# Four chunks' decays broadcast by TensorE, 256-column idle products in shorter gaps, and a new order of issue

## The chip, the cores and the metric

The kernel runs on one core of a Trainium2 chip. The metric is the device time of one execution in microseconds (us), of which three are given for the kernel before. TensorE is called PE here, VectorE DVE, ScalarE ACT, GpSimd POOL; SP issues nearly all DMAs.

## The reference

Three stages follow one another on 4 batches of 768 tokens with 8 heads of 32. Cut to what matters:

```python
# 1: chunked state space scan (per head; N = 16 states, D = 32)
cum = np.cumsum(log_a, axis=-1); L = np.exp(cum_i - cum_j) * causal   # decays
y  = (C @ B.T * L) @ x + (C @ state) * np.exp(cum)
state = decay_full * state + sum_j decay_from_j * B_j x_j
# 2: x of all heads side by side, 256 wide
xn = (x - mean) / sqrt(var + 1e-6) * g_ln
x  = x + relu(xn @ w_ch1) @ w_ch2                  # 256 -> 1024 -> 256
# 3: mix along the sequence with rank 32, then a second such network
u = x + (x.T @ U @ V).T
out = u + relu(u @ w_ch1) @ w_ch2
```

## The kernel before, in words

**Work.** Tokens are handled in chunks of 128: 6 chunks per batch, numbered k = 0 to 23 over all batches. In the first two batches a chunk is cut in two halves of 64 tokens (`NS = (2, 2, 1, 1)`). The two networks take the tokens in groups of 256 (chunks 0 and 1 of a batch) and 512 (chunks 2 to 5).

**A chunk's chain** (function `chunk`). The decays a of chunk k must stand on all partitions as the tile `lt`; `bc` brings them there. A scan on DVE (line 677) turns `lt` into the products of decays. PE forms C·B (`cb`, two chunks at a time), DVE multiplies both (`mm`, line 701), DVE or POOL scales B by the last decay (`bw`, line 719), PE forms the chunk's state (`sps`), DVE carries it on (`gst`) and masks it (`stm`, line 805), and PE puts all together in `yps` (lines 754 and 763). ACT and DVE split that into a high and a low part (`yhl`), PE transposes a copy (`tps`), and ACT takes mean and variance from it.

**How the decays get to all partitions.** Lines 464 to 479 load the rows of chunks 2 to 23 once (`rows`), clip them on DVE (line 462), let POOL set the first of each chunk to zero, and store them in DRAM as `arows`. For every chunk from the third on, `bcast` loads from there with a broadcast: two DMAs of 64 partitions in the first batches. `lt` has three buffers, one of which first holds `rows`. For chunks 0 and 1 (`if k < 2`, line 622) another way is taken: two small loads put the raw rows on a few partitions (tile `r`), DVE clips and splits them in two float32r parts (`rh`), and one pair of products per chunk with a selecting matrix `selr` puts them on all partitions in PSUM (`bcp`, line 615), where the scan reads them.

**Weights.** They come as 64-bit words (`raw`, 512 KB a piece; three buffers). ACT and DVE make float32 of them (ACT lines 268 and 369, DVE line 373 twice: the merges) and split them into a high and a low part. For the first matrix of network 1, PE also takes out the mean with four products `pc` (line 396) and one more (line 409). A token group times a high and low weight needs six products `hps` (line 928); ACT and DVE split its relu (`hh` line 935, `hl` line 939), and six or twelve products `acc` (lines 953 and 959) follow.

**What sets the order.** Everything is one list per engine, written out by a planner (`Plan.issue`): each item has a cost, its predecessors and a due time, and the planner plays them through with constants for cost (`LAT`, `RATE`, ...), shifts of due times (`SHIFT`) and `T0`, `PER` for the networks. The engines then run these lists in order; what an item really waits for is a semaphore. A queue is never overtaken: a DVE instruction that waits holds all that stand behind it.

**Idle products.** Where the planner sees a gap on PE it puts in products of zeros (`filler`, in the trace `dummy`), which wait for nothing and give nothing:

```python
while n != "dummy" and now < WARM[2] and t - now > WARM[3]:
    self.filler()
```

`WARM` gives the planned time from which they may stand, the time up to which they are costed double, the time after which there are none, and the gap above which they are put in.

Of the kernel before, what the change touches and what calls it, by code (L numbers as in the profile page):

```python
# [8 lines left out]
F32 = mybir.dt.float32  # L9
F32R = mybir.dt.float32r  # L10
# [3 lines left out]
ALU = mybir.AluOpType  # L14
# [3 lines left out]
C = 128  # L18
NC = S // C
XW = DM + H * N  # L20
NK = B * NC
# [3 lines left out]
WARM = (1.0, 8.0, 60, 1.0)  # L25
EARLIEST = {'warm': 62.0, ('cb', 0, 0): 6.0, (('w1', 0, 0), 'ld'): 3.2}
# [4 lines left out]
FIRST = [('bc0', 0), ('bcl', 0), ('sel', 0), ('sel', 1), 'cst0', ('ra', 0, 0), ('rcb', 0, 0), ('stk', 0), ('xb', 0), (('w1', 0, 0), 'ld'), 'cst', 'rows',  # L31
# [4 lines left out]
POOL = {'rac': (), 'bw': (3, 4), 'stm': (4, 2)}  # L36
PE_SPLIT = ()
# [6 lines left out]
LAT, PER, T0, NEAR, SWITCH, STAY = 0.298, 1.0526, 11.79, 0.2, 0.046, 3.07  # L44
# [9 lines left out]
RATE, FLIGHT = 282, 8  # L54
# [5 lines left out]
SHIFT = dict(zip("rows w0 w1 w2 ra0 ra chunk0 chunk".split(), [-0.37, 1.36, 0.67, 13.48, -4.54, -9.02, -1.53, -2.91]))  # L60
# [16 lines left out]
class Plan:  # L77
# [35 lines left out]
    def issue(self):  # L113
# [45 lines left out]
        while left:  # L159
# [21 lines left out]
            if eng == "PE":  # L181
                now = max(free[eng], WARM[0])
                while n != "dummy" and now < WARM[2] and t - now > WARM[3]:
                    self.filler()
                    step = dict(words=2, cost=0.216 if now > WARM[1] else 0.43)
                    now = max(now, self.fetched(step))
                    self.ran(step, now)
                    now += step["cost"]
                t = max(t, self.fetched(it))
                self.ran(it, t)  # L190
# [38 lines left out]
def mamba_ffn_mixer(ctx: ExitStack, tc: tile.TileContext, a_rows, a_rep, cbT, xb,  # L229
# [37 lines left out]
    def copy(out, in_, **kw):  # L267
        A.activation(out=out, in_=in_, func=AF.Copy, **kw)  # L268
# [25 lines left out]
    stk = {}  # L294
# [280 lines left out]

    def chunk(k):
# [30 lines left out]
        def ld_first_rows():  # L607
            for j in range(2):
                load(out=pair["r"][32 * j:32 * j + 2], in_=a_rows[j:j + 1].rearrange("k (i x) -> (k i) x", i=2))
# [12 lines left out]
        if k < 2:  # L622
            if k == 0:
                pair["r"] = y_p.tile([128, 512], F32, tag="uhl0", name="r2")
                pair["sel"] = y_p.tile([128, 2, C], F32R, tag="uhl1", name="selr")
                pair["h"] = y_p.tile([128, 2, 512], F32R, tag="yhl1", name="rh")
                sl_ = pair["sel"]
                add(("bcz", k), "DVE", 0.3, lambda: V.memset(pair["r"], 0.0), due=-3e3)
                add(("selz", k), "DVE", 0.17, lambda: V.memset(f32(sl_)[:, 1, :], 0.0))
                add(("sel", 0), "ACT", act(C), lambda: copy(sl_[:, 0, :], sel), ["cst0", "table"])  # L630
                add(("sel", 1), "ACT", act(C), lambda: copy(sl_[32:64, 1, :], sel[0:32]), ["cst0", "table", ("selz", k)])
                add(("bc0", k), "SP", sp(2, 8), ld_first_rows, [("bcz", k)])
                add(("bc1", k), "DVE", dve2(512), lambda: clip(pair["r"]), [("bc0", k)])
# [6 lines left out]
        else:  # L640
            gone = [x for j in ((0, 1) if k in (3, 4) else (k - 3,)) for x in
# [29 lines left out]
        def scan(hf):  # L671
            if k == 0:
                pair[2] = att_p.tile([128, 1024], F32, tag="lt", name="lt", bufs=3)
            if k < 2:
                lt[k] = pair[2][:, 512 * k:512 * (k + 1)]
            t = lt[k][:, hf * 512:(hf + 1) * 512]
            V.tensor_tensor_scan(t, pair[k] if k < 2 else t, eye, 0.0, op0=ALU.mult, op1=ALU.add)  # L677
# [24 lines left out]
        for hf in range(parts):  # L702
            add(("scan", k, hf), "DVE", scn(512), lambda hf=hf: scan(hf), [("bc", k), ("eye", ns)] + [("scan", 0, 0)] * (k == 1),
                frees=[("bc", k)] * (k < 2))
# [403 lines left out]
    def bank():  # L1108
# [4 lines left out]
    plan.filler = lambda: P.matmul(dummy[0], zeros[:, :C], zeros.rearrange("p (o i) -> p o i", o=1).to_broadcast([128, 2, 2 * C]),  # L1113
                                   start=True, stop=True)
# [52 lines left out]
```

## Time and profile before

| | us |
|---|---|
| time, median of 3 runs (371.94, 375.89, 377.66) | 375.89 |
| the profiled execution's own time | 375.81 |
| its span, first to last instruction | 374.0 |
| PE busy | 361.4 (97%) |
| DVE busy | 244.0 (65%) |
| ACT busy | 169.5 (45%) |
| mean granted share of the TensorE clock | 0.982 |

The profile is of one execution. The 1.8 us between its time and its span lie before the first and after the last instruction. A busy PE is not PE at its peak: a product that runs at half the clock is busy twice as long.

### The profile page before, as it was taken

The numbers are of one execution on the slowest core, as the hardware profiler recorded it, in microseconds if no ns is written. First come the engines' busy times: TensorE is split into PE (matmuls) and PEld (weight loads), VectorE is DVE, ScalarE is ACT, GpSimd is POOL, SyncE is SP. The second block draws the span as 40 slices with busy tenths as digits, with TensorE's granted clock in tenths as the row PEclk, the third lists the DMA queues.
The fourth block names the chain that finished last, engine by engine and source line by source line (L and its number), as shares of the span: only waits on it lengthen the run. The fifth ranks groups of instructions, "written<-read, shape, count | busy, mean of one in ns | idle before, by whom it ended". The sixth has DMA issues, their size and how long they took to land.

```text
span 374.0 us, 8463 instructions
## 1 busy us (share of the span) xinstructions
PE 361.4 (97%) x3377; PEld 306.8 (82%) x3377; DVE 244.0 (65%) x523; ACT 169.5 (45%) x473; POOL 9.3 (2%) x27
## 2 busy tenths in 40 slices
PE   7898799999999999999999999999999999999996
PEld 3476698989878789899887689998978788998896
DVE  6869789999995693896462796458952742434242
ACT  3473784677962642433432551225442551244221
POOL 4001100000100000000000000000000000000000
PEclk9599989999999999999999999999999999999999
DMA  5858862746380425791220435019200100000010
GB/s 149 248 169 224 261 191 60 205 137 202 106 322 20 144 78 154 215 355 40 64 85 0 147 101 152 4 46 270 92 26 0 58 3 0 2 0 30 0 57 30
DMA packets 31973, 41.58 MB, mean 111 GB/s; under 512 B 4170, under 2 KB 21370, under 8 KB 31934
## 3 DMA queue, kind: packets, MB, share of 16 engines
q1 hardware_dynamic: 31502, 40.67, 35.7%
q8 instruction: 27, 0.44, 0.5%
q10 hardware_dynamic: 432, 0.37, 0.3%
q14 instruction: 12, 0.10, 0.1%
HBM read 33.07 MB, written 7.95 MB: 110 GB/s over the span
## 4 chain that ended last, share of the span: by engine, by line
PE 84%; DVE 5%; DMA 5%; ACT 1%; issue 1%; SPq 1%; POOL 1%; DVEq 0%; ACTq 0%; POOLq 0%
PE hps L928 34%; PE acc L959 18%; PE acc L953 15%; PE pc L396 2%; DMA xt<-in_xb 2%; PE yps L742 2%; PE yps L754 2%; PE cb L694 2%; PE ups L1040 2%; DMA rows<-in_a_rows 1%; PE tps L856 1%; DMA raw<-in_w 1%; SPq L253 1%; PE gps L1001 1%; PE yps L763 1%
## 5 line engine op out<-in xcount | busy, mean ns | idle before, releaser
L939 DVE SCALAR_TENSOR_TENSOR hl<-hps,hh 128x256 fp32r<-128x256 f32 (+1 forms) x128 | 70.6, 552 | 92.9 <-ACT hh L935 92.7
L935 ACT ACTIVATE hh<-hps 128x256 fp32r<-128x256 f32 (+1 forms) x128 | 62.6, 489 | 138.8 <-PE hps L928 130.8
L928 PE MATMUL hps<-yhl,w 128*128 128x512 f32 (+1 forms) x384 | 79.1, 344 | 1.2 <-ACT w L268 0.6
L928 PE MATMUL hps<-uhl,w 128*128 128x256 f32 (+1 forms) x384 | 77.7, 339 | 0.0
L959 PE MATMUL acc<-hh,w 128*128 128x512 f32 (+1 forms) x256 | 73.8, 340 | 0.0
L953 PE MATMUL acc<-w,hh 128*128 128x256 f32 x384 | 73.1, 286 | 0.2 <-DVE w L271 0.2
L928 PEld LDWEIGHTS hps<-yhl,w 128*128 128x128 f32 x384 | 59.9, 192 | 10.1 <-ACT w L268 1.3
L928 PEld LDWEIGHTS hps<-uhl,w 128*128 128x128 f32 x384 | 60.8, 189 | 8.4 <-ACT u L268 0.4
L953 PEld LDWEIGHTS acc<-w,hh 128*128 128x128 f32 x384 | 62.0, 192 | 3.8 <-issue 0.8
L953 PE MATMUL acc<-w,hl 128*128 128x256 f32 x192 | 54.6, 284 | 0.0
L959 PEld LDWEIGHTS acc<-hh,w 128*128 128x128 f32 x256 | 46.1, 189 | 5.9 <-issue 1.0
L677 DVE TENSOR_TENSOR_SCAN lt<-lt,eye 128x512 f32<-128x512 f32 x34 | 41.0, 1214 | 4.3 <-DMA lt<-arows 4.3
L959 PE MATMUL acc<-hl,w 128*128 128x512 f32 (+1 forms) x128 | 43.2, 337 | 0.1
L953 PEld LDWEIGHTS acc<-w,hl 128*128 128x128 f32 x192 | 37.0, 192 | 0.0
L959 PEld LDWEIGHTS acc<-hl,w 128*128 128x128 f32 x128 | 24.2, 189 | 2.6 <-DVE hl L939 0.3
L701 DVE TENSOR_TENSOR mm<-cb,lt 128x512 f32<-128x512 f32 x36 | 23.6, 683 | 1.5 <-PE cb L694 1.0
L268 ACT ACTIVATE w<-raw 128x512 f32<-128x512 f32 (+2 forms) x19 | 12.2, 643 | 16.6 <-DMA raw<-in_w 10.2
L268 ACT ACTIVATE yhl<-yps 128x128 fp32r<-128x128 f32 x48 | 11.1, 274 | 15.6 <-PE yps L763 8.6
L271 DVE TENSOR_TENSOR yhl<-yps,yhl 128x128 fp32r<-128x128 f32 x48 | 11.6, 285 | 4.8 <-ACT yc L268 2.2
L369 ACT ACTIVATE raw<-raw,half 128x512 int32<-128x512 uint16 (+2 forms) x19 | 13.9, 734 | 0.0
L373 DVE SCALAR_TENSOR_TENSOR w<-w,raw 128x512 int32<-128x512 int32 (+2 forms) x19 | 12.3, 655 | 1.6 <-PE pc L409 1.1
L373 DVE SCALAR_TENSOR_TENSOR w<-raw,w 128x512 int32<-128x512 int32 (+2 forms) x19 | 12.3, 650 | 0.0
(111 smaller groups left out, 357.3 us busy)
## 6 DMA issues: line engine op xcount, KB each, us to landing
raw<-in_w SPq DMA_DIRECT2D x16, 512.0 KB, 5.0
lt<-arows SPq DMA_DIRECT2D x12, 512.0 KB, 5.3
stk<-st SPq DMA_DIRECT2D x48, 96.0 KB, 2.7
st<-sh SPq DMA_DIRECT2D x8, 384.0 KB, 4.3
xt<-in_xb SPq DMA_DIRECT2D x14, 192.0 KB, 4.1
lt<-arows SPq DMA_DIRECT2D x20, 128.0 KB, 3.7
out<-u SPq DMA_DIRECT2D x8, 256.0 KB, 2.1
xt<-in_xb SPq DMA_DIRECT2D x20, 96.0 KB, 3.4
```

Of the source, the lines that this page charges most:

```text
L268: A.activation(out=out, in_=in_, func=AF.Copy, **kw)
L271: eng.tensor_tensor(out=out, in0=in0, in1=in1, op=ALU.subtract)
L369: A.activation(out=words(0), in_=cell["r"][:rows, :2 * n].bitcast(U16).rearrange("p (n w) -> p n w", w=4)[:, :, 1], func=AF.Identity, scal ...
L373: V.scalar_tensor_tensor(out=cell["t"].bitcast(I32), in0=a(), scalar=scalar, in1=b(), op0=op, op1=ALU.bitwise_or)
L396: P.matmul(p[:, o * 256:(o + 1) * 256], (gd if o == k else gm)[:, k, :], t()[:, k, :], start=(o == k == 0), stop=False, skip_group_check=True)
L677: V.tensor_tensor_scan(t, pair[k] if k < 2 else t, eye, 0.0, op0=ALU.mult, op1=ALU.add)
L701: V.tensor_tensor(out=mm_[k][:, s_], in0=cbp[k, hf], in1=lt[k][:, s_], op=ALU.mult)
L928: P.matmul(p[:, :n], w[:, k, fs], x[:, k, :], start=(i == 0), stop=(i == 5))
L935: A.activation(out=hh[:, :n], in_=hps[l, key, f][:, :n], func=AF.Relu)
L939: V.scalar_tensor_tensor(out=hl[:, :n], in0=hps[l, key, f][:, :n], scalar=0.0, in1=f32(hh[:, :n]), op0=ALU.max, op1=ALU.subtract)
L953: P.matmul(p, x[:, t * C:(t + 1) * C], w[:, f, :], start=(f == 0 and i == 0 and t % 2 == 0), stop=(f == NF - 1 and i == 2), skip_group_che ...
L959: P.matmul(accs[l, key][d][:, :n], w[:, f, ds_], x[:, :n], start=(f == 0 and i == 0), stop=(f == NF - 1 and i == 2))
```

## The change

One load of eight rows of 512 replaces the two small loads; tile `r` then holds chunks 0 to 3, and `selr` selects for four chunks (two ACT copies out of an identity matrix instead of two out of a stored pattern; the memset of `selr` goes). Chunks 2 and 3 take their decays from `bcp` too: four more products, and their four broadcast DMAs go. The pairs (0, 1) and (2, 3) each share a buffer of `lt`, and `before` names the chunks that must be done before a buffer is used again. The idle products have 256 columns instead of 512, fill gaps above 0.6 us (planned) instead of 1.0, and end at 28 us planned instead of 60. The constants of cost and due times are others, so all lists have another order.

```diff
-WARM = (1.0, 8.0, 60, 1.0)
-EARLIEST = {'warm': 62.0, ('cb', 0, 0): 6.0, (('w1', 0, 0), 'ld'): 3.2}
+WARM = (1.0, 6.0, 28, 0.6)
+EARLIEST = {'warm': 30.0, ('cb', 0, 0): 6.0, (('w1', 0, 0), 'ld'): 3.2}
...
+ROWS = 4
...
-LAT, PER, T0, NEAR, SWITCH, STAY = 0.298, 1.0526, 11.79, 0.2, 0.046, 3.07
+LAT, PER, T0, NEAR, SWITCH, STAY = 0.287, 1, 13.09, 0.115, 0.056, 3.07
...
-RATE, FLIGHT = 282, 8
+RATE, FLIGHT = 251, 8
...
-SHIFT = dict(zip("rows w0 w1 w2 ra0 ra chunk0 chunk".split(), [-0.37, 1.36, 0.67, 13.48, -4.54, -9.02, -1.53, -2.91]))
+SHIFT = dict(zip("rows w0 w1 w2 ra0 ra chunk0 chunk".split(), [-1.78, -6.02, 1.38, 12.04, -3.04, -11.46, -1.31, -2.87]))
...
-                    step = dict(words=2, cost=0.216 if now > WARM[1] else 0.43)
+                    step = dict(words=2, cost=0.109 if now > WARM[1] else 0.216)
...
+    def before(k):
+
+        tiles = [()] + [(j, j + 1) for j in range(0, ROWS, 2)] + [(j,) for j in range(ROWS, NK)]
+        at = next(i for i, t in enumerate(tiles) if k in t)
+        return tiles[at - 3] if at >= 3 else ()
...
         def ld_first_rows():
-            for j in range(2):
-                load(out=pair["r"][32 * j:32 * j + 2], in_=a_rows[j:j + 1].rearrange("k (i x) -> (k i) x", i=2))
+            load(out=pair["r"][:2 * ROWS], in_=a_rows[:ROWS].rearrange("k (i x) -> (k i) x", i=2))
...
-        if k < 2:
+        if k < ROWS:
...
-                add(("selz", k), "DVE", 0.17, lambda: V.memset(f32(sl_)[:, 1, :], 0.0))
-                add(("sel", 0), "ACT", act(C), lambda: copy(sl_[:, 0, :], sel), ["cst0", "table"])
-                add(("sel", 1), "ACT", act(C), lambda: copy(sl_[32:64, 1, :], sel[0:32]), ["cst0", "table", ("selz", k)])
-                add(("bc0", k), "SP", sp(2, 8), ld_first_rows, [("bcz", k)])
-                add(("bc1", k), "DVE", dve2(512), lambda: clip(pair["r"]), [("bc0", k)])
+                for j in range(0, ROWS, 2):
+
+                    add(("sel", j), "ACT", act(2 * C), lambda j=j: copy(
+                        sl_[:, 2 * j:2 * j + 4], eye64[:, 2 * j:2 * j + 4].rearrange("p (k o) -> p k o", o=1).to_broadcast([128, 4, w_])),
+                        ["cst0", "table"])
+                    alias["sel", j + 1] = ("sel", j)
+                add(("bc0", k), "SP", sp(1, 16), ld_first_rows, [("bcz", k)])
+                add(("bc1", k), "DVE", dve2(512), lambda: clip(pair["r"][:64]), [("bc0", k)])
...
-            V.tensor_tensor_scan(t, pair[k] if k < 2 else t, eye, 0.0, op0=ALU.mult, op1=ALU.add)
+            V.tensor_tensor_scan(t, pair[k] if k < ROWS else t, eye, 0.0, op0=ALU.mult, op1=ALU.add)
...
-    plan.filler = lambda: P.matmul(dummy[0], zeros[:, :C], zeros.rearrange("p (o i) -> p o i", o=1).to_broadcast([128, 2, 2 * C]),
-                                   start=True, stop=True)
+    plan.filler = lambda: P.matmul(dummy[0][:, :256], zeros[:, :C], zeros, start=True, stop=True)
```

Three places of the lists follow; a line is source line, operation, what it writes and reads.

DVE, the stretch in which the state of chunks 0 and 1 (`gst`, `stm`), the clip of `rows` and the first weight's merges stand; before:

```order
L796 SCALAR_TENSOR_TENSOR gst<-gst,df,sps 128x64
L701 TENSOR_TENSOR mm<-cb,lt 128x512
L462 TENSOR_SCALAR rows<-rows 88x256
L805 TENSOR_TENSOR stm<-gst,cst 128x128
L796 SCALAR_TENSOR_TENSOR gst<-gst,df,sps 128x64 x2
L701 TENSOR_TENSOR mm<-cb,lt 128x512
L340 SCALAR_TENSOR_TENSOR gd<-cst,gm 128x128 x2
L373 SCALAR_TENSOR_TENSOR w_218<-w_218,raw_158 128x512
L805 TENSOR_TENSOR stm<-gst,cst 128x128
L373 SCALAR_TENSOR_TENSOR w_218<-raw_158,w_218 128x512
L271 TENSOR_TENSOR yhl<-yps,yhl 128x2x64 x2
```

and with the change:

```order
L805 SCALAR_TENSOR_TENSOR gst<-gst,df,sps 128x64
L710 TENSOR_TENSOR mm<-cb,lt 128x512
L814 TENSOR_TENSOR stm<-gst,cst 128x128
L463 TENSOR_SCALAR rows<-rows 88x256
L805 SCALAR_TENSOR_TENSOR gst<-gst,df,sps 128x64 x2
L341 SCALAR_TENSOR_TENSOR gd<-cst,gm 128x128
L374 SCALAR_TENSOR_TENSOR w_252<-w_252,raw_164 128x512
L341 SCALAR_TENSOR_TENSOR gd<-cst,gm 128x128
L374 SCALAR_TENSOR_TENSOR w_252<-raw_164,w_252 128x512
L686 SCALAR_TENSOR_TENSOR lt<-bcp,eye 128x512
L814 TENSOR_TENSOR stm<-gst,cst 128x128
```

The first `stm` now stands ahead of the clip of `rows`, both `mm` of this pair are done before it, and the scan of chunk 2 (`lt<-bcp`) stands between the merges and the second `stm`; the scan of chunk 3 follows four rows on.

PE, from the idle products behind the first chunk's `yps` to the first weight's products `pc` (line 409 is that weight's fifth product); before:

```order
L1113 MATMUL dummy<-zero 128x512
L1113 LDWEIGHTS zero
L1113 MATMUL dummy<-zero 128x512
L754 MATMUL yps<-ra,stm 32x64 x16
L763 MATMUL yps<-mm,xt_93 32x64 x16
L396 MATMUL pc<-w_218,gd 128x256
L396 MATMUL pc<-w_218,gm 128x256 x2
L396 MATMUL pc<-w_218,gd 128x256
L689 MATMUL cb<-stp 64x128 x16
L856 MATMUL tps<-cst,yc 128x128 x4
L409 MATMUL pc<-w_372,negi 128x512
```

and with the change, from `pc` on:

```order
L397 MATMUL pc<-w_252,gd 128x256
L397 MATMUL pc<-w_252,gm 128x256 x2
L397 MATMUL pc<-w_252,gd 128x256
L763 MATMUL yps<-ra,stm 32x64 x16
L772 MATMUL yps<-mm,xt_93 32x64 x16
L865 MATMUL tps<-cst,yc 128x128 x2
L410 MATMUL pc<-w_372,negi 128x512
L1122 LDWEIGHTS zero
L1122 MATMUL dummy<-zero 128x256
```

`pc` now stands ahead of the second chunk's `yps`; a second idle product, the next pair's `cb` and then the first `hps` follow the last row shown. Idle products: 9 ahead of `bcp`, then 1, 3, 2 and 2 before; with the change 17, then 9 ahead of `sps`, 11 behind it, 9 ahead of `pc`, 2, and 11 behind the third `sps`, all of half the columns.

SP, the loads from the store of `arows` on (`stp` is what `cb` reads); before:

```order
L253 DMA arows<-rows 88x256
L253 DMA xt_93<-in_xb 64x384 x2
L253 DMA raw_370<-in_w 128x2x512
L253 DMA stp<-in_cbT 32x4x128
L253 DMA stp<-in_cbT 16x4x128 x2
L253 DMA stp<-in_cbT 32x4x128
L253 DMA stp<-in_cbT 16x4x128 x2
L253 DMA lt<-arows 64x512 x6
L253 DMA xt_93<-in_xb 64x384 x2
L253 DMA raw_478<-in_w 128x2x512
L253 DMA xt_93<-in_xb 64x384 x2
L253 DMA raw_495<-in_w 128x2x512
```

and with the change, from the same store on:

```order
L254 DMA arows<-rows 88x256
L254 DMA stp<-in_cbT 32x4x128
L254 DMA stp<-in_cbT 16x4x128 x2
L254 DMA stp<-in_cbT 32x4x128
L254 DMA stp<-in_cbT 16x4x128 x2
L254 DMA xt_93<-in_xb 64x384 x2
L254 DMA lt<-arows 64x512 x2
L254 DMA raw_544<-in_w 128x2x512
L254 DMA xt_93<-in_xb 64x384 x2
L254 DMA lt<-arows 64x512 x2
L254 DMA xt_93<-in_xb 64x384 x2
L254 DMA raw_587<-in_w 128x2x512
```

The six broadcast loads of chunks 2 to 4 have become two (chunk 4 alone); the next two are those of chunk 5, and the last `xt` row shown is that of chunk 5. Before, one more set of `stp`, the loads of `lt` of chunk 5 and two more pieces of weights stood between the last row shown and the `xt` of chunk 5. Counted over the whole list up to the `xt` of chunk 5, SP issues 8 pieces of weights, 8 broadcast loads and 4 sets of `stp` before, and 5, 4 and 3 with the change.

## Rows read from the trace of the kernel before

**Rows 1.** the profile's page, part 1: busy time, share of the span, instructions

```profile
PE 361.4 (97%) x3377; PEld 306.8 (82%) x3377; DVE 244.0 (65%) x523; ACT 169.5 (45%) x473; POOL 9.3 (2%) x27
```

**Rows 2.** windows: length, then busy us of each engine, granted clock, DMA share, GB/s

```profile
9.50:19.70 10.20, 8.52 (x154) 5.29 (x155) 8.35 (x26) 4.34 (x13) 0.45 (x4) 0.50 0.78 233
19.70:47.00 27.30, 23.26 (x408) 18.05 (x407) 21.27 (x47) 18.36 (x52) 2.90 (x4) 1.00 0.78 223
47.00:50.40 3.40, 3.40 (x38) 3.17 (x41) 3.05 (x8) 2.53 (x8) 0.00 (x0) 0.51 0.71 171
56.00:100.00 44.00, 43.66 (x568) 38.69 (x570) 42.63 (x90) 30.34 (x72) 0.33 (x2) 1.00 0.48 145
```

**Rows 3.** windows, VectorE alone: busy us, granted clock, DMA share, GB/s

```profile
13.00:60.30 47.30, 39.43 (x86) 0.89 0.70 197
```

**Rows 4.** waits of VectorE, 13 to 60.4 us: total, times, longest

```profile
DVE lt L677 <- DMA lt<-arows: 2.3, 3, 1.0
DVE yhl L271 <- ACT yc L268: 1.4, 2, 1.2
DVE hl L939 <- ACT hh L935: 1.3, 3, 0.6
...
DVE bw L719 <- DMA xt<-in_xb: 1.2, 1, 1.2
DVE w L373 <- PE pc L409: 1.1, 1, 1.1
```

**Rows 5.** chain that ended last: start us, us, what

```profile
7.42 5.57 DMA rows<-in_a_rows
...
17.56 3.03 PE pc L396 x8
...
25.18 1.73 PE pc L396 x8
...
39.36 5.52 DMA xt<-in_xb
...
53.68 1.40 PE hps L928 x6
```

**Rows 6.** timeline of VectorE: start us, us, instructions, idle before and who ended it

```profile
6.46 1.22 DVE L677 TENSOR_TENSOR_SCAN lt<-bcp,eye 128x512 f32<-128x512 f32 x1 [1.07 <-PE bcp L615]
...
13.01 0.29 DVE L462 TENSOR_SCALAR rows<-rows 88x256 f32<-88x256 f32 x1 [1.29 <-DMA rows<-in_a_rows]
...
13.43 0.59 DVE L796 SCALAR_TENSOR_TENSOR gst<-gst,df,sps 128x64 f32<-128x64 f32 x2
...
14.53 0.61 DVE L340 SCALAR_TENSOR_TENSOR gd<-cst,gm 128x128 f32<-128x128 f32 x2
15.05 0.68 DVE L373 SCALAR_TENSOR_TENSOR w<-w,raw 128x512 int32<-128x512 int32 x1
...
16.46 0.48 DVE L271 TENSOR_TENSOR yhl<-yps,yhl 128x128 fp32r<-128x128 f32 x2
...
17.58 0.42 DVE L462 TENSOR_SCALAR ra<-ra 128x512 f32<-128x512 f32 x1
...
27.69 1.22 DVE L677 TENSOR_TENSOR_SCAN lt<-lt,eye 128x512 f32<-128x512 f32 x1 [0.58 <-DMA lt<-arows]
29.56 1.23 DVE L677 TENSOR_TENSOR_SCAN lt<-lt,eye 128x512 f32<-128x512 f32 x1 [0.65 <-DMA lt<-arows]
30.70 0.27 DVE L719 TENSOR_TENSOR bw<-xt,lt 128x128 f32<-128x128 f32 x1
...
39.94 1.23 DVE L677 TENSOR_TENSOR_SCAN lt<-lt,eye 128x512 f32<-128x512 f32 x1 [1.04 <-DMA lt<-arows]
```

**Rows 7.** timeline of TensorE, the same columns

```profile
10.88 1.46 PE L1113 MATMUL dummy<-zero 128*128 128x512 bf16 x3
13.65 0.65 PE L754 MATMUL yps<-ra,stm 32*32 32x64 f32 x16 [1.31 <-DVE stm L805]
...
23.49 1.69 PE L928 MATMUL hps<-yhl,w 128*128 128x256 f32 x12 [0.61 <-ACT w L268]
```

## What the change will do to the time

> **What bounds the kernel now.** The page's first part is read first: PE is busy 361.4 of 374.0 us [rows 1], so the end is set by PE, and only a stretch where PE does less than it could has anything to give. The windows show where that is. From 56 us to 100 PE is busy 43.66 of 44.00 us at the full clock, and DVE 42.63 of 44.00 beside it [rows 2]: there both engines go at the pace of the work. Ahead of it they don't. From 19.7 to 47 us PE is busy 23.26 of 27.30 us, and two stretches show the lower clock of 1.2 GHz: 9.5 to 19.7 us (granted 0.50) and 47.0 to 50.4 (0.51) [rows 2]. So the change is won or lost ahead of 56 us, and what it wins there moves all that follows, since nothing behind has room to absorb it or to add to it.
>
> Who bounds that early part? The reader should look at DVE alone: from 13.0 to 60.3 us it is busy 39.43 of 47.30 us, idle 7.87 [rows 3]. Its work there is a list in fixed order (merges of weights, scans, splits) that PE's products wait for. What ended its idle times: the broadcast loads `lt` 2.3 us, ACT's copies 1.4, ACT's relu 1.3, the inputs `xt` 1.2, PE's `pc` 1.1 [rows 4]. The chain of waits tells the same: it leads over the DMA of `rows` (5.57 us), the first `pc` (3.03 us at the lower clock, 1.73 for the next one at the higher), the DMA of `xt` from 39.36 to 44.88, and reaches the first 512-column `hps` at 53.68 [rows 5].
>
> **The change part by part.** The sum is made against the profiled execution's 375.81 us, 0.08 below the median shown.
>
> *The first load and `bcp`.* One load less is issued, and DVE loses the memset of `selr`, ahead of its wait for that load: 0. Four more `bcp` products of 512 columns come behind the first `cb`. Cover: there PE waits for DVE's first state. Taken as 0; uncovered, they have two thirds of the columns of the row of twelve `hps` of 1.69 us [rows 7], so 0 to 1.1 us.
>
> *Two scans read PSUM instead of SBUF.* The trace has both kinds at the same form: 1.22 us from `bcp` in PSUM, 1.22 and 1.23 us from `lt` in SBUF [rows 6]. So 0. Against this stands the Trainium skill, Perfetto Trace Analysis, section Optimizing Scalar/DVE Operations, which gives DVE about 60 ns of overhead per access to SBUF and about 125 to PSUM: by that the two scans would cost 0.13 us more, an estimate, and the sum below would be 371.9. The trace does not show it.
>
> *The order on DVE up to the first `hps`.* Before, DVE stands at the clip of `rows` until 13.01 us, with the first `stm` behind it, so the first `yps` starts at 13.65 [rows 6, 7]. Now `stm` stands ahead of the clip. Behind the clip I add up starts to starts: clip and `stm` row to `gst` 0.2 (13.22 less 13.01), `gst` 0.5, `gd` 0.52, first merge 0.6, second merge 0.68 to its end: 13.01 + 2.5 = 15.5 us. Before, `pc` began at 17.56 [rows 5], since a chunk's `yps` stood ahead of it. PE must by then have done the first `yps` and 9 idle products; three of 512 columns take 1.46 us at the lower clock [rows 7], so one of half the columns at twice the clock takes 0.12 us, and with `stm` 1.3 us sooner they end by 14.5. So `pc` starts at 15.6 and, at the higher clock, takes 1.73 us: done at 17.3 instead of 20.6. What is late next is DVE: two scans (1.14 each, start to start [rows 6]), `stm` 0.2, two splits `yhl` of 0.5, a merge and its second half 1.2, a clip 0.4 stand ahead of the first group's last `yhl`: 15.4 + 5.1 = 20.5. So the first `hps` starts at 20.6 instead of 23.49 [rows 7]: 2.9 us sooner. That is no term by itself, since the scans done by then are missing later; it says that PE does not spoil what DVE gains.
>
> *The DMAs.* All loads of the early part go through SP in order. Four broadcast loads of 128 KB go. Up to the inputs of chunk 5 there are 4 such loads, 3 pieces of weights of 512 KB and a set of `stp` (256 KB) less: 2.36 MB, which at the 223 GB/s of this stretch [rows 2] is 10.6 us. Before, they landed at 44.88 [rows 5]; now about 34.3. For `lt` of chunk 5 it is 1.31 MB, 5.9 us: 34.0 instead of 39.9 [rows 6].
>
> *DVE's idle time with the change.* The waits of chunks 2 and 3 for `lt` go: 0.58 and 0.65 [rows 6]. The wait for `xt` of chunk 5, 1.2, goes. Chunk 5's scan waited 1.04 for `lt`; in the new list DVE has from 20.5 two scans of 1.14, nine operations of 512 columns at 0.6 (as the merges) and some 3.4 us of small ones ahead of it, so it reaches it at 31.6 and may wait 2.4; it waits less if the queue runs faster than its mean, in which DMAs were busy 0.78 of the time. Bounds 0 and 2.4; I take 2.0, nearer to the mean rate, which is the row. ACT and PE held DVE for 1.4 + 1.3 + 1.1 = 3.8 us [rows 4]; with the first products 2.9 us earlier and the `pc` at full clock some of it goes: bounds 0 and 3.8, and I take half, 1.9, as no row tells which of these waits are late ACT and which are DVE's being early. Left: 3.9 instead of 7.87, a gain of 4.0 us.
>
> *Idle products.* 31 of them lie between the first `cb` and the first `hps` (9, 11, 9, 2), 11 behind the third state: at 0.12 us each 3.7 and 1.3 us, where PE waits for DVE for longer. Taken as 0; if that cover is gone, see the second rival.
>
> *All that follows 56 us.* The lists differ little there, and both engines are full [rows 2]: 0. If PE finds one chunk late there, it is a wait of the size of a scan, 1.2 us.
>
> Sum: 375.81 - 4.0 = 371.8 us, 1.1% below. In PE's terms: 1.7 us of the gain is what the stretch at 1.2 GHz from 47.0 to 50.4 cost (half of 3.40 us), 1.3 the `pc` at half clock, the rest idle time.
>
> **The rivals.** *All of DVE's idle time goes.* The queue is faster than its mean, ACT and PE keep up: the gain is 7.87, the time 367.9. For it: the inputs of chunk 5 come 10 us sooner, and the lower clock held ACT and PE back in two stretches. Against it: a list in fixed order hardly ever runs without a wait, and three engines feed it.
>
> *The idle products hold up real work (slower).* They wait for nothing, so if the clock stays at 1.2 GHz from 9.5 us on, as it was before with 5 idle products there, each takes 0.24 us. PE has done the first states at 10.9 [rows 7]; 11 idle products bring it to 13.6. From the first `yps` to the first `hps` it needed 9.84 us (23.49 less 13.65 [rows 7]), most of it at the lower clock and with 4 idle products of 512 columns in it; the same work with 11 of 256 columns takes 0.7 us more. The first `hps` then starts at 24.1, so the 2.9 us and 0.6 more are lost. At that clock the last 11 idle products cost 1.3 us more, and the next two `pc` 1.3 each. Time: 371.8 + 3.5 + 1.3 = 376.6, and 379.2 with the `pc`; taken 378. It decides whether the granted clock of 9.5 to 19.7 us is near 0.5 or near 1. Before, PE stood idle there until 13.65 for DVE [rows 7], which the new list removes. The Trainium skill, TensorE: Matmul & The Clock Gate, Part 1, says that the lower clock is the default and that activity lifts it; by that this rival would not occur, the trace agrees for 19.7 to 47 us (1.00, PE busy 23.26 of 27.30 [rows 2]), while from 47.0 to 50.4 PE is busy throughout at 0.51 [rows 2].
>
> *Given back on DVE.* Only the 1.23 us of chunks 2 and 3 are saved; chunk 5's `lt` is waited for in full (2.4), and ACT and PE hold DVE as before (3.8): 6.2 us idle instead of 7.87, 374.1 us. For it: bytes of weights ahead of the last merges are nearly the same, and ACT's list is the same length.
>
> **How the numbers follow.** Chances: forecast 0.42, all idle time gone 0.25, given back 0.20, idle products in the way 0.13. The time is that of the likeliest, 371.8, whose own range is 370 to 373.5. The range reaches from 367.5, below the first rival by what the runs scatter, to 378.0, to the middle of the second: low tail 0.07 and high tail 0.08 are left out. Two per cent, about what a measurement of this kernel can tell from no change, are 7.5 us: 368.4 and 383.4. Faster takes most of the first rival and a little of the forecast: 0.20. Slower by that much needs the second rival and a chunk that comes late several times behind 56 us: 0.03. Within: 0.77.
>
> **What would show it.** Right: the first `hps` near 20.6 us, `pc` of 1.7 us each, granted clock near 1 from 9.5 us on, DVE's idle time from 13 to 57 us near 4 us with one wait for `lt` of chunk 5, the first 512-column `hps` near 49.5, PE full from there. Wrong: first `hps` past 23 with a clock near 0.5; DVE idle near 7; or PE idle behind 56 us, which none of these steps holds.

## The result, and the profile after

| | before | with the change |
|---|---|---|
| median, us (four runs each) | 375.71 | 371.21 |
| lowest and highest | 371.94, 377.66 | 370.03, 372.79 |
| the profiled execution's own time | 375.81 | 370.03 |
| its span | 374.0 | 368.2 |
| mean granted clock | 0.982 | 0.998 |

The ratio is 0.9891, 95% interval 0.9848 to 0.9934. Run twice more beside its variants the changed kernel stood at 0.9841 (0.9797 to 0.9885) and 0.9861 (0.9818 to 0.9904) of the kernel before. So 4.1 to 6.0 us are gained, 1.1 to 1.6%: faster, and by less than 2% in each of the three (one interval reaches 2.0). The forecast was 371.8, a gain of 4.0.

The page's first part, against [rows 1]:

```profile
PE 359.3 (98%) x3423; PEld 307.9 (84%) x3423; DVE 243.6 (66%) x522; ACT 170.0 (46%) x473; POOL 9.0 (2%) x27
```

The same windows as in [rows 2] (busy us of PE, weight loads, DVE, ACT, POOL, then clock, DMA share, GB/s):

```profile
9.50:19.70 10.20, 8.95 (x209) 6.57 (x211) 9.63 (x25) 5.98 (x15) 0.84 (x4) 1.00 0.83 239
19.70:47.00 27.30, 25.43 (x479) 20.86 (x470) 23.48 (x53) 21.31 (x69) 1.95 (x4) 1.00 0.79 222
47.00:50.40 3.40, 3.40 (x20) 2.89 (x19) 3.40 (x10) 1.68 (x6) 0.33 (x2) 1.00 0.63 143
56.00:100.00 44.00, 43.95 (x612) 38.69 (x611) 42.84 (x92) 34.02 (x82) 1.85 (x2) 1.00 0.53 163
```

Both stretches of 1.2 GHz are gone, from 19.7 to 47 PE is busy 2.2 us longer (idle products are 1.4 us of it, before 0.6) and DVE 2.2, and behind 56 us it is as full as before. DVE alone, which answers to [rows 3], in three windows:

```profile
5.00:13.00 8.00, 6.59 (x18) 1.00 0.83 247
13.00:57.00 44.00, 40.18 (x88) 1.00 0.72 200
5.00:60.30 55.30, 50.02 (x109) 1.00 0.75 209
```

and the same three of the kernel before:

```profile
5.00:13.00 8.00, 5.41 (x12) 0.78 0.81 237
13.00:57.00 44.00, 36.13 (x81) 0.88 0.75 211
5.00:60.30 55.30, 44.84 (x98) 0.88 0.72 203
```

Up to 60.3 us DVE does 50.02 us of work instead of 44.84, 5.18 more. The profiled execution is 5.78 us shorter. In two more profiles of the changed kernel (experiment 5) DVE does 3.50 and 3.43 us more up to 60.3 us, and those executions are 4.26 and 5.01 us shorter. The waits of the first profile, against [rows 4] (13 to 60.4 us; total, times, longest; the whole list):

```profile
DVE lt L686 <- DMA lt<-arows: 1.7, 1, 1.7
DVE vrq L903 <- ACT vrq L894: 0.7, 1, 0.7
DVE yhl L272 <- ACT yhl L269: 0.3, 1, 0.3
DVE w L374 <- ACT raw L370: 0.3, 1, 0.3
DVE mm L710 <- PE cb L698: 0.2, 1, 0.2
DVE hl L948 <- ACT hh L944: 0.2, 1, 0.2
```

One wait for `lt` is left. DVE's timeline, against [rows 6], says which: chunk 4's at 29.20; chunk 5's, at 33.67, finds its data there. The first `stm` now waits for a DMA of constants, 0.50:

```profile
12.01 0.29 DVE L814 TENSOR_TENSOR stm<-gst,cst 128x128 f32<-128x128 f32 x1 [0.50 <-DMA cst<-in_consts]
...
14.65 1.22 DVE L686 TENSOR_TENSOR_SCAN lt<-bcp,eye 128x512 f32<-128x512 f32 x1
...
16.97 1.21 DVE L686 TENSOR_TENSOR_SCAN lt<-bcp,eye 128x512 f32<-128x512 f32 x1
...
29.20 1.22 DVE L686 TENSOR_TENSOR_SCAN lt<-lt,eye 128x512 f32<-128x512 f32 x1 [1.67 <-DMA lt<-arows]
...
33.67 1.22 DVE L686 TENSOR_TENSOR_SCAN lt<-lt,eye 128x512 f32<-128x512 f32 x1
...
35.90 0.50 DVE L728 TENSOR_TENSOR bw<-xt,lt 128x128 f32<-128x128 f32 x1
```

TensorE's timeline, against [rows 7]:

```profile
7.74 1.20 PE L621 MATMUL bcp<-rh,selr 128*128 128x512 f32 x4
...
12.45 0.43 PE L763 MATMUL yps<-ra,stm 32*32 32x64 f32 x16 [0.62 <-DVE stm L814]
...
14.88 0.67 PE L397 MATMUL pc<-w,gd 128*128 128x256 f32 x2 [0.53 <-DVE w L374]
...
19.99 0.98 PE L937 MATMUL hps<-yhl,w 128*128 128x256 f32 x6
...
28.03 0.43 PE L787 MATMUL sps<-xt,bw 128*32 128x64 f32 x16 [1.26 <-POOL bw L728]
28.39 0.70 PE L397 MATMUL pc<-w,gd 128*128 128x256 f32 x2
...
46.86 1.55 PE L937 MATMUL hps<-yhl,w 128*128 128x512 f32 x6
```

The chain of waits, against [rows 5]. The DMA of `rows` and the late `xt` at 39.36 are off it; in their place stand a piece of weights and, from 24.09, the `xt` on which POOL's `bw` and the product at 28.03 depend. Behind 28.03 the chain of this profile holds only PE's products up to 79 us, but for 0.57 us in which PE waits for nothing that the profile shows: by this chain PE sets the pace there, no longer DVE.

```profile
6.05 5.33 DMA raw<-in_w
14.88 1.97 PE pc L397 x8
24.09 3.32 DMA xt<-in_xb
28.46 1.92 PE pc L397 x8
```

### The profile page after: what moved, and what is told of

The parts are those of the page before. It is cut to its first block, busy times and chain, and to the rows that moved or that the text cites. A ratio compares the mean times of both kernels' runs of the same rounds, so it can differ in the third digit from the quotient of the medians.

```text
span 368.2 us, 8542 instructions
## 1 busy us (share of the span) xinstructions
PE 359.3 (98%) x3423; PEld 307.9 (84%) x3423; DVE 243.6 (66%) x522; ACT 170.0 (46%) x473; POOL 9.0 (2%) x27
## 4 chain that ended last, share of the span: by engine, by line
PE 84%; DVE 6%; DMA 5%; ACT 2%; SPq 1%; issue 1%; POOL 1%; DVEq 0%; POOLq 0%
PE hps L937 35%; PE acc L968 18%; PE acc L962 16%; PE tps L865 2%; PE pc L397 2%; DMA raw<-in_w 1%; PE yps L763 1%; DMA lt<-arows 1%; DVE w L374 1%; PE cb L703 1%; PE yps L751 1%; PE ups L1049 1%; SPq L254 1%; PE cb L698 1%; PE yps L772 1%
## 5 line engine op out<-in xcount | busy, mean ns | idle before, releaser
L937 PE MATMUL hps<-yhl,w 128*128 128x512 f32 (+1 forms) x384 | 78.2, 341 | 0.0
L686 DVE TENSOR_TENSOR_SCAN lt<-lt,eye 128x512 f32<-128x512 f32 x32 | 38.7, 1214 | 3.6 <-DMA lt<-arows 3.6
```

The lines of the kernel that those rows point to most:

```text
L686: V.tensor_tensor_scan(t, pair[k] if k < ROWS else t, eye, 0.0, op0=ALU.mult, op1=ALU.add)
L937: P.matmul(p[:, :n], w[:, k, fs], x[:, k, :], start=(i == 0), stop=(i == 5))
```

## The experiments

My theory was that of the prediction: DVE's list bounds the start, what it no longer waits for is gained one to one, and fewer bytes in the queue are a good part of that. The rivals: the granted clock (by the idle products) makes the gain, or the new order alone does.

**1. The kernel before with the new idle products, lists unchanged.** The planner goes on with its own figures, and a second count beside it puts out the products, so that no other row moves.

```diff
+                SHOWN = (1.0, 6.0, 28, 0.6)
+                at_ = now
+                while n != "dummy" and at_ < SHOWN[2] and t - at_ > SHOWN[3]:
+                    self.filler()
+                    at_ += 0.109 if at_ > SHOWN[1] else 0.216
                 while n != "dummy" and now < WARM[2] and t - now > WARM[3]:
-                    self.filler()
...
-    plan.filler = lambda: P.matmul(dummy[0], zeros[:, :C], ..., start=True, stop=True)
+    plan.filler = lambda: P.matmul(dummy[0][:, :256], zeros[:, :C], zeros, start=True, stop=True)
```

> The kernel before with every list unchanged (DVE, ACT, SP, POOL row for row, PE but for the idle products); only the idle products are those of the change: 256 columns, gaps above 0.6 us, up to 28 us planned: 20, 5, 9, 7 and 8 instead of 9, 1, 3, 2 and 2 of 512 columns. My theory (DVE's fixed list bounds the start, the clock is a small part): the granted clock of 9.5 to 19.7 us rises from 0.50 to near 1, the first pc goes from 3.03 to about 1.73 us, all waits of DVE for lt and xt stay; the first hps is at most 1.3 us sooner than 23.5, and 0 to 1.3 us of time is gained: 0 to a third of the 4.5 between the two kernels. Rival (the clock makes the gain): 3 us or more are gained. Rival (idle products in the way): the clock stays near 0.5 and the time grows by 1 us or more.

Measured: 378.23 against 377.20, ratio 1.0042 (1.0008 to 1.0075). Nothing is gained, but the clock as a whole did not rise either (mean 0.981). The low stretch has moved:

```profile
9.50:19.70 10.20, 5.55 (x161) 4.12 (x162) 6.71 (x20) 4.24 (x13) 0.44 (x4) 0.93 0.84 239
19.70:28.00 8.30, 8.30 (x54) 6.07 (x53) 4.98 (x9) 4.06 (x13) 0.00 (x0) 0.50 0.61 168
```

```profile
18.83 0.42 PE L767 MATMUL yps<-mm,xt 64*32 64x64 f32 x2 [2.42 <-issue]
```

The granted clock is 0.93 up to 19.7 us, but PE is busy only 5.55 of 10.20 us there: it waits for DVE's states, and at 18.83, in the middle of a chunk's `yps`, it has stood 2.42 us for nothing that the profile shows ("issue"). So `pc` starts at 19.18, later than the 17.56 of before, though DVE is done with that weight's second merge at 15.95; and `pc` and the first `hps` then stand at a clock of 0.50. More idle products did not keep the clock up in these lists. The third case, idle products in the way, comes nearest, with 1.6 us by the ratio, though by a low clock that comes later than it said.

So this variant cannot say what a full clock would give. Single executions on record say a little: one of the kernel before, beside experiment 9, had a mean clock of 0.999 and took 374.99 us, where that kernel's median is 376.41 and the changed kernel's 370.84; one of this variant had 0.998 and took 376.05. Single runs scatter by more than such differences, but neither comes near the changed kernel. With experiment 7 this speaks against the clock as the whole gain; a smaller part of it is not excluded.

**2. The changed kernel with the idle products of before, lists unchanged.** The same means the other way round: 22 products of 512 columns instead of 59 of 256.

> The changed kernel with every list unchanged but for the idle products, which are placed by the rule of before: 512 columns, gaps above 1.0 us: 8, 3, 4, 3, 0 and 4 instead of 17, 9, 11, 9, 2 and 11 of 256. The columns are nearly the same in number, so if the clock stays near 1.0 from 9.5 to 19.7 us as in the changed kernel, the time is the changed kernel's within 0.5 us, and the size of the idle products was worth nothing. If the clock falls to 0.5 there, pc and the first yps take twice as long: first hps 1.3 to 3 us later, time 1.3 to 3 us more. Rival (the clock makes the gain): all of 4.5 us are lost.

Measured: 369.21, ratio 0.9810 (0.9763 to 0.9858). And in a second set of runs, beside the changed kernel on one chip:

> The changed kernel with the idle products by the rule of before on unchanged lists, now beside the changed kernel. If 22 products of 512 columns do as well as 59 of 256 (or better), as the profile of the first run of it says (DVE and PE meet again at 28 us), it is 0 to 2 us faster than the changed kernel. If the clock matters, it is 1.3 us or more slower.

370.24 against the changed kernel's 370.84, ratios 0.9835 (0.9794 to 0.9876) and 0.9861: no worse, and a difference of 0.6 us that the intervals don't tell. The first of the two profiles is the instructive one. Its clock is 0.83 from 9.5 to 19.7 us, and most of `pc` runs at half speed:

```profile
9.50:19.70 10.20, 7.91 (x164) 5.14 (x162) 9.15 (x22) 4.61 (x12) 0.84 (x4) 0.83 0.82 235
```

```profile
15.14 1.19 PE L401 MATMUL pc<-w,gd 128*128 128x256 f32 x2 [0.87 <-DVE w L378]
16.13 1.91 PE L401 MATMUL pc<-w,gm 128*128 128x256 f32 x4
...
21.07 0.98 PE L941 MATMUL hps<-yhl,w 128*128 128x256 f32 x6
...
28.00 0.43 PE L791 MATMUL sps<-xt,bw 128*32 128x64 f32 x16
28.36 0.70 PE L401 MATMUL pc<-w,gd 128*128 128x256 f32 x2
...
46.69 1.55 PE L941 MATMUL hps<-yhl,w 128*128 128x512 f32 x6
```

The first `hps` is 1.1 us later than in the changed kernel, yet the `sps` that needs POOL's `bw` starts at 28.00 instead of 28.03, the next `pc` at 28.36 instead of 28.39. PE had 1.26 us to spare there for the transfer of `xt`, and 1.43 in the third profile of the changed kernel. In the second, PE stands 1.19 us at 19.05 for nothing that the profile shows, and reaches this product at 27.97 all the same. The time (369.21) is even 0.8 below that of the changed kernel's profile.

**3. The changed kernel with the 17 first idle products only.** The other 42 are not put out.

```diff
-                    self.filler()
+                    if now < 5.0:
+                        self.filler()
```

> The changed kernel with the 17 idle products ahead of bcp alone; the 42 behind (9, 11, 9, 2, 11) are left out, all other rows as they are. My theory: they cost nothing while they stand, so without them the time can only grow, by what the clock falls to: if it goes to 0.5 between 9.5 and 19.7 us, pc takes 3.0 instead of 1.9 us and the first hps comes 1.3 to 3 us later, time 1 to 3 us more. Rival (the idle products are in the way of real work): the time falls by up to 2 us with the first yps and sps sooner. If the clock stays near 1 without them: no difference.

Measured: 369.80, ratio 0.9827 (0.9783 to 0.9870). The clock falls, as expected, to 0.67 from 9.5 to 19.7 us (PE busy 6.30 of 10.20), and the time does not grow (the changed kernel itself: 0.9841 and 0.9861). So the 42 products neither cost nor give anything that shows here.

**4. The changed kernel, scans of chunks 2 and 3 made twice.**

```diff
+            for _ in range(2 if k in (2, 3) else 1):
-            V.tensor_tensor_scan(t, pair[k] if k < ROWS else t, eye, 0.0, ...)
+                V.tensor_tensor_scan(t, pair[k] if k < ROWS else t, eye, 0.0, ...)
```

> The changed kernel in which DVE makes the scans of chunks 2 and 3 twice (the same result from the same PSUM bank): 2.44 us of work more on DVE at 15 to 20 us, nothing else changed. My theory (DVE's list bounds the part ahead of 56 us): the first hps is 2.4 us later than 19.99; of this, chunk 4's wait for lt (1.67 us at 29.2) takes up as much as the DMA isn't late with it, so the time grows by 0.8 to 2.4 us. Rival (PE's own work or the DMAs bound the start): the time grows by under 0.4 us.

Measured: 371.92, ratio 0.9894 (0.9848 to 0.9940). On that chip experiments 2 and 3 had 369.21 and 369.80, so it is 2.1 to 2.7 us slower than these, which have other idle products. Against the changed kernel's own 0.9841 and 0.9861, measured on another chip, it is 1.2 to 2.0 us slower, with intervals that overlap. Its timeline of DVE shows some 2.5 us come in (2.47 and 2.48 us for two scans each, instead of 1.22 and 1.21) and part of them go again:

```profile
15.06 2.47 DVE L687 TENSOR_TENSOR_SCAN lt<-bcp,eye 128x512 f32<-128x512 f32 x2
18.63 2.48 DVE L687 TENSOR_TENSOR_SCAN lt<-bcp,eye 128x512 f32<-128x512 f32 x2
...
30.11 1.22 DVE L687 TENSOR_TENSOR_SCAN lt<-lt,eye 128x512 f32<-128x512 f32 x1
```

The scan of chunk 4 stands at 30.11 without a wait, against 29.20 with 1.67 us of waiting: the wait took up what it could. The first 512-column `hps` is at 48.09, 1.2 us after that of the changed kernel's first profile and 0.3 after that of its third. So work added to DVE's list at 15 to 20 us reaches the end in part, and a wait for a DMA in that list is slack for what stands ahead.

**5. The changed kernel again, twice.**

> The changed kernel itself, run beside the others so that they can be compared with it on one chip. If its own idle products cost nothing, it stands to before as the variants with the old idle products (0.981) or with the first 17 alone (0.983) did: 0.980 to 0.984. If they hold up work, it stays at 0.989, 2 to 3 us above these.

371.23, ratio 0.9841: at the edge of the first case. And beside experiments 2 (second part), 9 and 10:

> The changed kernel, beside the next three on one chip, so that differences of 1 to 2 us between it and its variants can be told: 0.984 to 0.989 of before.

370.84, ratio 0.9861: between the two cases, so that a small cost of the idle products stays open. The wait for chunk 4's `lt` is not always there in the same size: 1.67, 0.50 and 1.95 us in the three profiles. DVE is idle 5.43 and 5.33 us from 13 to 57 us in these two, against 3.82 in the first.

**6. The changed kernel with `ROWS = 2`** (two chunks' decays by TensorE as before; new constants and idle products).

```diff
-ROWS = 4
+ROWS = 2
```

> The changed kernel with ROWS = 2: chunks 2 and 3 get their decays by the broadcast loads again (four DMAs of 128 KB, 0.52 MB more ahead of chunk 4's); constants and rule of idle products are the new ones; the planner orders the lists anew. Theory A (the decays without DMA are what gains): DVE's waits for lt come back, 0.6 us each as before and the later loads 2.3 us later (0.52 MB at 223 GB/s): 2 to 4 us slower than the changed kernel. Theory B (the new constants, that is the order, gain): within 1 us of the changed kernel.

Measured: 378.22, ratio 1.0048 (1.0020 to 1.0076): 7 us slower than the changed kernel, slower than before. The profile is of the slowest of its twelve runs (379.31). DVE is busy 33.27 us of 13 to 57 (before 36.13):

```profile
26.48 0.42 DVE L948 SCALAR_TENSOR_TENSOR hl<-hps,hh 128x256 fp32r<-128x256 f32 x1 [2.55 <-ACT hh L944]
...
49.74 1.22 DVE L686 TENSOR_TENSOR_SCAN lt<-lt,eye 128x512 f32<-128x512 f32 x1 [2.65 <-DMA lt<-arows]
```

Theory B (the order alone) falls. Theory A named the sign and the waits for `lt`, but gave half the size; the wait of 2.55 us for ACT was in neither theory.

**7. The changed kernel with the constants of before** (four chunks' decays and new idle products).

```diff
-LAT, PER, T0, NEAR, SWITCH, STAY = 0.287, 1, 13.09, 0.115, 0.056, 3.07
+LAT, PER, T0, NEAR, SWITCH, STAY = 0.298, 1.0526, 11.79, 0.2, 0.046, 3.07
...
-RATE, FLIGHT = 251, 8
+RATE, FLIGHT = 282, 8
...
-SHIFT = ...[-1.78, -6.02, 1.38, 12.04, -3.04, -11.46, -1.31, -2.87]))
+SHIFT = ...[-0.37, 1.36, 0.67, 13.48, -4.54, -9.02, -1.53, -2.91]))
```

> The changed kernel with the constants of before (LAT, PER, T0, NEAR, SWITCH, RATE and SHIFT); the decays of four chunks on TensorE and the new idle products stay; the planner orders the lists anew. Theory A (decays): at most 1.5 us slower than the changed kernel. Theory B (order): 3 us or more slower, that is near the time of before. Sign of B in the trace: the weights of the second matrix and the xt of chunk 5 land as late as before (44.9 us) and DVE waits for them.

Measured: 375.96, ratio 0.9982 (0.9953 to 1.0010): the time of before, and 4.7 us above the changed kernel. That is the size of theory B, but its sign is missing: DVE does not wait for `xt`. The profile is again of the slowest run (379.17). Its clock is 1.00 through all of the first 70 us, so that a full clock there is not what gains. DVE waits 4.3 us for `lt` (three times), and PE stands still for the states of the second batch's end:

```profile
77.71 0.43 PE L763 MATMUL yps<-ra,stm 32*32 32x64 f32 x16 [2.78 <-DVE stm L814]
```

**8. The kernel before with four chunks' decays** (constants and idle products of before; the diff of experiment 7 and that of the idle products together).

> The kernel before with the decays of four chunks on TensorE; constants and idle products as before; the planner orders the lists anew. Theory A (decays): 2 to 4 us faster than before, DVE without a wait for lt of chunks 2 and 3. Theory B (order): within 1 us of before, DVE's idle time of 13 to 60 us still near 7 us, now for other things. If both parts are needed together, this one and the one with the old constants are both near the time of before.

Measured: 379.91, ratio 1.0095 (1.0058 to 1.0132): slower than before. The waits for `lt` of chunks 2 and 3 are gone, and five others stand there, of 4.8 us in all; the same stall of PE comes at 79.6:

```profile
DVE lt L686 <- DMA lt<-arows: 4.8, 5, 1.1
```

```profile
79.61 0.54 PE L763 MATMUL yps<-ra,stm 32*32 32x64 f32 x24 [1.89 <-DVE stm L814]
```

So theory A falls as well in its simple form: the decays alone gain nothing. With the new constants they do: two chunks' decays by TensorE give 378.22 us, four 371.23, and six 371.52 (experiment 10).

**9. The changed kernel with the bytes put back.** Four broadcast loads of 128 KB ahead of chunk 4's, into a buffer in DRAM (before they went into `lt`); no other row changes.

```diff
+            if k == ROWS:
+                spare = dram.tile([256, 512], F32, name="spare", bufs=1)
+                for i in range(4):
+                    load(out=spare[64 * i:64 * i + 64], in_=a_dram[...].to_broadcast([64, 512]))
```

> The changed kernel with the four broadcast loads of 128 KB put back into the queue at the place ahead of chunk 4's lt, into a spare buffer in DRAM that nobody reads; all lists else unchanged, no wait added. My theory (fewer bytes in the queue are part of the gain): what stands behind them lands 2.3 us later (0.52 MB at 223 GB/s), POOL's bw of chunk 4, which releases PE at 28.03, and the scan of chunk 4 come later by that, and the time grows by 1.5 to 2.4 us. Rival (the bytes were hidden; the gain is in the order of DVE's list): less than 0.5 us.

Measured: 374.64, ratio 0.9941 (0.9902 to 0.9980), against 370.84 (0.9861) beside it: 3.0 to 3.8 us slower. SP, DVE and PE show the way of it:

```profile
25.26 3.20 SPq L254 DMA_DIRECT2D spare<-arows  x4
28.50 1.23 SPq L254 DMA_DIRECT2D lt<-arows  x2
```

where the profile of the changed kernel beside it has

```profile
25.17 2.09 SPq L254 DMA_DIRECT2D lt<-arows  x2
```

```profile
32.38 1.23 DVE L691 TENSOR_TENSOR_SCAN lt<-lt,eye 128x512 f32<-128x512 f32 x1 [4.05 <-DMA lt<-arows]
```

```profile
34.57 0.86 PE L768 MATMUL yps<-ra,stm 32*32 32x64 f32 x24 [2.57 <-DVE stm L819]
...
51.90 1.55 PE L942 MATMUL hps<-yhl,w 128*128 128x512 f32 x6
```

```profile
27.00:34.20 7.20, 4.35 (x68) 3.01 (x66) 3.11 (x10) 1.19 (x2) 0.41 (x1) 1.00 0.68 201
34.20:41.00 6.80, 6.43 (x90) 5.53 (x91) 4.24 (x12) 4.18 (x14) 1.13 (x2) 0.50 1.05 245
```

DVE's wait for chunk 4's `lt` is 4.05 us instead of 1.95 in the profile beside it: 2.1 more for 0.52 MB, as the queue's mean rate said (2.3). But SP's rows give another reason of the same size. SP takes 3.20 us to issue the four loads, so it is done with issuing chunk 4's `lt` at 29.73 instead of 27.26, 2.5 us later, and from there to the scan it is 2.65 us against 2.70. So the delay is there as soon as SP has issued the load. Whether the bytes or the number of loads make it was not tried. The change itself saves both: in the kernel before, the six `lt` loads of chunks 2 to 4 took SP 4.70 us to issue, and the two left with the change take 1.94. POOL's `bw`, which the expectation also named, is not late (27.90, beside it 27.95): it stands ahead of the added loads.

PE then idles 2.57 us, and behind that its clock is 0.50 from 34.2 to 41.0 us, with real work on it. More is lost than the 1.5 to 2.4 us expected, and it goes with the clock: by their mean clock the twelve runs are 371.27 us at 1.000, 372.99 to 373.80 at 0.993 to 0.995, 373.97 to 376.65 at 0.989 to 0.991. The one run at 1.000 is 0.4 us above the changed kernel's median and within its range (370.24 to 372.26), so the added loads without the low clock may cost hardly anything. How much of the loss is the clock and how much longer waits in the same runs is not told apart.

**10. Six chunks' decays by TensorE, idle products of before**, a candidate.

```diff
-ROWS = 4
+ROWS = 6
...
```

The rest of its edit is that of experiment 2.

> A candidate to beat both: ROWS = 6, so that chunks 4 and 5 too get their decays by TensorE, with the idle products by the rule of before; the planner orders the lists anew with the constants of the change. If removed DMAs and waits for lt are what gains, 1 to 2 us faster than the changed kernel (0.5 to 1.7 us of waits for lt of chunk 4 and 0.52 MB less). If the constants fit only the lists for which they were found, as the runs with one part each say, it is 2 to 6 us slower than the changed kernel.

Measured: 371.52, ratio 0.9873 (0.9830 to 0.9917): the changed kernel's time within the intervals, so neither of the two cases expected, without any wait for `lt` of chunks 4 and 5. The first `yps` now waits longer for the constants' DMA (1.28 at `stm`), and `pc` starts at 16.73 instead of 14.88. No version that was run is shown to beat the changed kernel.

**What the experiments say together.** For kernels with the changed kernel's lists, the table gives DVE's work from 5 to 60.3 us, the start of the first 512-column `hps` and the profiled execution's own time:

| lists of the changed kernel | DVE's work, us | first 512-column `hps`, us | time, us | time less `hps` |
|---|---|---|---|---|
| as it is, three profiles | 50.02, 48.34, 48.27 | 46.86, 46.85, 47.80 | 370.03, 371.55, 370.80 | 323.17, 324.70, 323.00 |
| idle products of before, two | 50.23, 49.08 | 46.69, 47.76 | 369.21, 370.91 | 322.52, 323.15 |
| first 17 idle products | 49.64 | 47.25 | 369.98 | 322.73 |
| scans twice | 51.14, of which 2.5 added | 48.09 | 371.30 | 323.21 |
| bytes put back | 44.21 | 51.90 | 375.64 | 323.74 |

What is lost or won ahead of 47 us stays to the end, as far as one profile of each can show: over 5 us of spread in the `hps` column the last one moves by 1.2, and by 2.2 with the one profile in which PE waits 0.90 us at 53.5 for a weight, behind waits of DVE of 0.77 and 1.08 us for DMAs. Most of the 5 us is one kernel, that with the bytes put back; without it and the late weight it is 1.4 us against 0.7.

DVE's work accounts for most of the gain and not for all of it. Against the one profile of the kernel before (44.84 us and 375.81), each of these executions is 0.6 to 1.6 us shorter than DVE's own work, without the added scans, would make it. The part that they have in common may lie in that one profile.

## Why the prediction was right, point by point

- **What bounds: DVE's list ahead of 56 us, one to one behind it.** In part. The second half holds within about 1 us in the table above. For the first, experiment 4 shows that 2.5 us more on DVE cost 1.2 to 2.7 us. But DVE's count falls short of the gain by 0.6 to 1.6 us, measured against one profile of the kernel before, and in the first profile the chain runs over PE alone from 28.03 us on. That DVE is the bound all the way to 56 us is not shown.
- **First load and added `bcp`: 0.** Right: they take 1.20 us at 7.74, and the first `yps` at 12.45 still waits 0.62 for DVE.
- **Scans from PSUM: 0.** Right: 1.22 and 1.21 us from `bcp`, 1.22 from `lt`. From the figures of the Trainium skill, Perfetto Trace Analysis, section Optimizing Scalar/DVE Operations, some 65 ns more for each would follow, an estimate; the trace does not show them.
- **Order on DVE, first `hps` 20.6.** Measured 19.99, and `pc` at 14.88 (15.6). From the clip to the end of the second merge it is the 2.5 us that I had added up (12.22 to 14.73); the clip itself comes sooner, since it has no wait until 13.01 any more. Each `pc` takes 1.97 and 1.92 us at the full clock, not 1.7. But what this would show was read too far: with the first `hps` at 21.07 and 21.89 (experiments 2 and 3) the time is the same.
- **DMAs.** Right to some tenths in when the loads land. The second piece of chunk 5's `xt` is issued at 30.5 and lands 3.8 us later, at 34.3 (forecast 34.3); the second piece of its `lt` at 29.1 and 4.4 later, at 33.5 (34.0). But bytes over a mean rate need not be the reason: of the 10.6 us by which this `xt` lands sooner, 8.9 are an earlier issue by SP (30.5 instead of 39.36). Experiment 9 does not tell bytes from the number of loads either, and its loss of 3 us or more goes with a low clock that the prediction did not have.
- **DVE idle 3.9 us.** Measured 3.82 from 13 to 57 in the first profile, and 5.43 and 5.33 in the other two: the match is of one profile. Its parts were others as well: chunk 5's scan was to wait 2.0 and waits 0; chunk 4's, to which I gave no wait, waits 1.67 (0.50 and 1.95 in other profiles) and so lets the data of chunk 5 arrive. ACT and PE hold DVE for 1.7 (1.9). That the sum of such parts is right is partly luck.
- **The size of the gain.** This is the term that was mis-sized. 4.0 was counted from 13.0 us on, and the wait of 1.29 us that ends at 13.01 [rows 6] was on the record, but not in the sum: `rows` stood ahead of the first `stm`. From 5 to 13 us DVE now does 6.59 us instead of 5.41 (6.47 and 6.29 in the other two profiles), 0.9 to 1.2 more. From 13.0 to 60.3 us it does 4.0 us more in the first profile, as forecast, and 2.4 and 2.5 in the others. With both, DVE gains 5.2, 3.5 and 3.4 us, and the executions are 5.78, 4.26 and 5.01 us shorter. So 371.8 is near the three medians (371.21, 371.23, 370.84) partly by luck: a term left out, a term that came in full only once, and some 0.6 to 1.6 us that are not in DVE's count and whose place no run shows.
- **Idle products: 0.** Right as far as it shows (experiments 2 and 3; a difference of 0.6 us is within the noise). The split of the gain "in PE's terms" was wrong: 1.3 us for `pc` at half the clock are worth nothing in these lists, since PE arrives early at the product at 28 us or has time to spare ahead of it. The rival of the idle products had a clock near 0.5 as its condition, and that did not occur: at 0.83 and 0.67 the stretch costs nothing that shows. Experiment 9 shows a low clock further back that goes with a loss.
- **First 512-column `hps` near 49.5.** Measured 46.86. The mark was badly chosen: before and after have other products ahead of it, so it can only be compared between kernels with the same lists.
- **Behind 56 us: 0.** Right for PE, which is busy 43.95 of 44.00 us (43.78 and 43.94 in the other two profiles).
- **What I did not see.** The sum treats the saved loads and the order as terms that add. Experiments 6 to 8 show that neither gains by itself (1.0048, 0.9982, 1.0095). In each of the three the planner gave other lists on PE, DVE, ACT and SP, and each of those lists has other waits, for `lt` and, in two of the three, a stall of 1.9 to 2.8 us at 78 to 80 us for DVE. The prediction was safe from this because it read the lists as built. Which constant matters for the four-chunk lists was not tried and stays open.

## What to carry to other kernels

In a kernel whose engines run fixed lists, count the work that the engine near the bound does up to the point where everything is full: most of the gain was in that count here. The window must begin where its first wait begins, not at a round number behind it, and one profile is not enough: the same kernel gave 3.4 to 5.2 us. The count fails where what follows is not full: with the lists of experiment 8, DVE did 2.02 us more than before up to 60.3 us, PE was busy 42.11 of 44.00 us behind 56, and the kernel was slower. A cheaper transfer pays through what stands behind it in the queue, not through its own wait alone. And a part of such a change can't be judged by leaving it out where a planner orders everything anew; keep the lists and change one thing in them.

## What the hardware showed that I had not expected

- A low clock can cost nothing that shows, or go with a loss, by where it falls. The same kernel had 0.83 and 1.00 from 9.5 to 19.7 us, with 369.21 and 370.91 us. From 34.2 to 41.0 us, behind 2.57 us in which PE stood idle, 0.50 went with a loss: 371.27 us in the one run with a mean clock of 1.000, 373.97 to 376.65 at 0.989 to 0.991.
- More idle products did not hold the clock where the lists left PE waiting: with 49 of 256 columns in the lists of before, the stretch at 0.50 only came later, from 19.7 to 28 us, behind 2.42 us in which PE stood idle, on real work, and the time was 0.4% longer.
- The issue of loads is a cost of its own. SP took 3.20 us to issue four broadcast loads of 128 KB; the load behind them was issued 2.5 us later and used 2.4 us later, with the same 2.7 us in between.
